# VectorE takes expert 1's branch, the output tiles are cleared by ScalarE and GpSimd in parts, and one written order runs to the end

## The chip, the cores and the metric

One Trainium2 chip, one of its cores. The number that counts is device time in microseconds (us) of one execution; it is given as the median of repeated runs. The core has five engines with instruction queues of their own: TensorE (PE; its weight loads are shown as PEld), VectorE (DVE), ScalarE (ACT), GpSimd (POOL) and SyncE (SP, which here only issues DMAs). Each engine works through its own queue in order, and engines wait for each other with semaphores. In the views of the profile a "q" behind an engine's name (ACTq) marks its sequencer: waits, register loads and branches, in which the engine computes nothing.

## What is computed

A retention layer (a recurrent linear attention with one decay per head) is followed by a mixture of eight experts, of which each token takes one. Cut to what matters:

```python
# attention: q, k, v are (4, 8, 768, 64); gamma = 1 - 2^(-5-h), scale = 1/8
for t in range(S):
    state = gamma * state + outer(k[t], v[t])
    y[t] = scale * q[t] @ state
x = y.transpose(0, 2, 1, 3).reshape(3072, 512)
# experts: w_gate (512, 8), w1 (8, 512, 1024), w2 (8, 1024, 512)
logits = x @ w_gate
expert = argmax(logits, axis=1)
gate_w = softmax(logits)[expert]
out[token] = gate_w[token] * (relu(x[token] @ w1[expert]) @ w2[expert])
```

Which tokens go to which expert is known only on the chip, at run time. All arithmetic that matters for time is float32.

## The kernel before, in words

**Attention and routing.** The first 434 to 735 lines work through 24 steps of 128 tokens. Each step writes its rows of `x` to a scratch array in DRAM (`x_d`), and the routing is worked out beside it: for each expert `e` a list of the rows it must fetch (`src`), of the rows of the output that it must write (`dst`), the gate factors, and the number of its tokens (`ne`). From `ne` comes `arm` (line 421): for each expert, a number that says how many blocks of 8 tokens above 256 it has.

**The early part of expert 0** (lines 737 to 788). The first 256 rows of expert 0 are gathered into `xs2[0]` and computed ahead of the general loop: layer 1 with 256 columns, then `pair` (line 341), which is layer 2 of two token tiles in seven instead of eight products. The result lies in `oa`, the first half of `xs2[0]` itself. Then come, on VectorE, the targets of these rows (`targets(*early, "_e")`, which ends in `dst_e`), the sixteen block transposes that turn the rows of expert 1 into columns (`turn(xs2[1], xT1, ...)`, line 209), and the targets of all rows (`dst`). GpSimd writes the early rows out (`scatter`, line 390).

**Memory that is handed on.** The pools `att` and `keep` of the attention end at line 789. The pools `mp` and `keep2`, which hold `hT`, the output tiles `o2[0]` and `o2[1]`, the second set of weights and the work tiles, take over their memory. So the first user of a new tile on each engine waits until the last user of the old pools is done; that is VectorE's last part of the early `pair` (line 355).

**The loop over the experts** (line 899). Expert `e` has its tokens in four tiles of 128. Three engines may take a branch for it (`tc.Switch`, line 929): there are 33 versions ("arms") of the code, one for each possible number of columns `n`, and a register with `arm[e]` picks one. `regs(e)` (line 406) loads the register; `fetch_ahead` (line 410) gives PE and ACT a hint of the coming arm. Before the change PE and ACT branch for every expert, and DVE from expert 2 on. In an arm lie layer 1 and the part of layer 2 that belongs to tiles 2 and 3 (`layer2`, line 227; for expert 0 the tiles 0 and 1 that the early part left over). After the arms comes `pair` for tiles 0 and 1, whose shape is always the same.

Layer 1 is `layer1` for experts 0 and 1 (line 220): for each of eight blocks `f`, PE makes a product in one of four PSUM buffers (`acc8[2 + f % 4]`), and ACT takes it through Relu into `hT`. So the product of block 4 can't start before ACT has emptied block 0. From expert 2 on it is `quarters1` (line 291), seven products for eight, with sums on DVE and the turns of the next expert spread between them (`spare`).

Beside each expert run: on DVE the sixteen turns of the next expert's rows (`turn`), the four sums of `h` that `pair` needs (`halves_of_h`, line 248, lines 253 to 256 in the profile), and the four sums of `x` for the next layer 1 (`halves_of_x`, line 289); on POOL the gathers of the rows of the expert after next, the scatters of finished rows, and the sums of the weights (`halves_of_w`, line 265; `halves_of_w1`, line 275); on SP the loads of the weights, 2 MB each (lines 150 and 155), into two homes in turn, each as soon as its old content has been used.

**The output tiles** are scattered whole, with rows beyond the expert's tokens sent nowhere. These rows must hold something defined, so both tiles are cleared once by POOL (lines 886 and 887) ahead of the loop.

**What sets the order.** Inside `tc.manual_schedule` the instructions of the named engines stay in the order in which the program writes them. Before the change there are two such stretches, one from line 700 to the end of the attention block, and one from line 885 on. At the seam a scheduler has mixed some instructions of both: ACT's and DVE's register loads stand early, the first clearing stands ahead of the early scatter on POOL, and six instructions of `dst` stand between the first turns of expert 2 on DVE.

Of the kernel before, what the change touches and what calls it, by code (L numbers as in the profile page):

```python
# [17 lines left out]
AF = mybir.ActivationFunctionType  # L18
# [3 lines left out]
P = 128  # L22
# [24 lines left out]
def middle(ap, n):  # L47

    dims = [list(d) for d in ap.ap]
    return bass.AP(tensor=ap.tensor, offset=ap.offset, ap=[dims[0], [0, n]] + dims[1:])  # L50
# [3 lines left out]
def kernel(  # L54
# [11 lines left out]
    nc = tc.nc  # L66
    B, H, S, D = q.shape
    N, DM = out.shape
# [7 lines left out]
    TC = W // P  # L76
# [10 lines left out]
    def ps(tag, bufs, name):  # L87
        return psum.tile([P, 512], F32, tag=tag, name=name, bufs=bufs)

    L = 32  # L90
    Q = P // L
# [6 lines left out]
    ident = const.tile([P, P], F32, tag="ident", name="ident")  # L98
# [54 lines left out]
    def weights2(pool, e):  # L153
        w2t = pool.tile([P, 1, FT, DM], F32, tag="w2t", name="w2t")
        nc.sync.dma_start(w2t, w2v[:, ds(e, 1), :, :])
        return w2t
# [7 lines left out]
    def gather(xs, idx, tiles, rows=N):  # L164
        for t in tiles:
            nc.gpsimd.indirect_dma_start(  # L166
                out=xs[:, t, :], out_offset=None, in_=x_d[0:rows, :],
                in_offset=bass.IndirectOffsetOnAxis(ap=idx[:, t : t + 1], axis=0), bounds_check=rows - 1,
                oob_is_err=False)
# [34 lines left out]
    def turns(xs, xT, tiles, which=range(Q * Q)):  # L204

        n = len(tiles)
        for i in which:
            r, g = divmod(i, Q)
            nc.vector.transpose(  # L209
                xT[ts(g, L), :, 0 : n * P].rearrange("p a (t r i) -> p r t a i", r=Q, i=L)[:, r, :, :, :],  # L210
                xs[ts(r, L), tiles[0] : tiles[0] + n, ts(g, P)].rearrange("p t (a i) -> p t a i", i=L))
            yield

    def turn(xs, xT, tiles, which=range(Q * Q)):
        for _ in turns(xs, xT, tiles, which):
            pass
# [3 lines left out]
    def layer1(n, xT, w1t, hT, f, tags=None):  # L220
        hp = (ps(*tags[f % len(tags)], "hp") if tags else acc8[2 + f % 4])[:, 0:n]
        for dt in range(DT):
            nc.tensor.matmul(hp, lhsT=w1t[:, 0, dt, ts(f, P)], rhs=xT[:, dt, 0:n], start=(dt == 0),  # L223
                             stop=(dt == DT - 1))
        nc.scalar.activation(out=hT[:, f, 0:n], in_=hp, func=AF.Relu)  # L225
# [22 lines left out]
    def halves_of_h(hT, hs, others=nc.vector):  # L248


        hs = [h.rearrange("p (f t) -> p f t", f=FH) for h in hs]
        a11, a12, a21, a22 = (hT[:, ts(j, FH), ts(i, P)] for i in range(2) for j in range(2))
        nc.vector.tensor_tensor(out=hs[0], in0=a21, in1=a22, op=ALU.add)
        nc.vector.tensor_tensor(out=hs[1], in0=hs[0], in1=a11, op=ALU.subtract)  # L254
        others.tensor_tensor(out=hs[3], in0=a12, in1=hs[1], op=ALU.subtract)
        others.tensor_tensor(out=hs[2], in0=a11, in1=a21, op=ALU.subtract)
        return hs
# [141 lines left out]
    PE, ACT, POOL, DVE, SP = (getattr(mybir.EngineType, nm) for nm in ("PE", "Activation", "Pool", "DVE", "SP"))  # L399
# [3 lines left out]
    HALF = EARLY // P  # L403
    ARMS = MOST - LEAST + 1

    def regs(e):
        return {g: nc.engines[g].value_load(arm[0:1, e : e + 1], min_val=0, max_val=ARMS - 1)
                for g in ((PE, ACT) if e < 2 else (PE, ACT, DVE))}

    def fetch_ahead(which, e):  # L410
        tc.switch_hint({g: which[g] for g in (PE, ACT)}, ARMS, label=f"job{e}")
# [22 lines left out]
    with ExitStack() as actx:  # L434
# [262 lines left out]
        LATE = len(steps) - 3  # L697
        for n in range(AHEAD):
            load(n)
        actx.enter_context(tc.manual_schedule(engines={PE, ACT, POOL, DVE, SP}))  # L700
        scale_v = scale(0)
        transpose(0)
        scale_v()
# [89 lines left out]
    o2 = [keep2.tile([P, TC, DM], F32, tag=f"o{i}", name=f"o{i}") for i in range(2)]  # L793
# [88 lines left out]
                layer2(W, hT, w2t, o2[E % 2], t, ogates[:, ts(j, TC)], iter(acc8[6 + t % 2 : 7 + t % 2]))  # L882
            scatter(o2[E % 2], odst[:, ts(j, TC)], range(TC))

    with tc.manual_schedule(engines={PE, ACT, POOL, DVE, SP}):
        for t in o2:
            nc.gpsimd.memset(t, 0.0)
        acc8.extend(ps(tag, n, f"p{i}") for i, (tag, n) in enumerate((("sc", 2), ("sc", 2), ("lg", 1)) + (("tr", 3),) * 3 + (("y", 2),) * 2))
        xT, xTn, rest = xTa, xT1, None
        s3 = [keep2.tile([P, 2, F // 2], F32, tag=f"s{i}", name=f"s{i}", bufs=1) for i in range(3)]  # L890
        T = [keep2.tile([P, 2, W // 2], F32, tag=f"t{i}", name=f"t{i}", bufs=1) for i in range(4)]
        hs = [keep2.tile([P, FH * P], F32, tag=f"hs{i}", name=f"hs{i}", bufs=1) for i in range(4)]
        ws = [keep2.tile([P, FH * DH], F32, tag=f"ws{i}", name=f"ws{i}", bufs=1) for i in range(4)]
        temps = [[keep2.tile([P, W // 2], F32, tag=f"q{k}{i}", name=f"q{k}{i}", bufs=1) for i in range(2)] for k in range(3)]
        turn_of = keep2.tile([P, 1], F32, tag="turn_of", name="turn_of", bufs=1)
        of_pair = dict(m10=temps[0][0], m11=temps[0][1], u20=temps[1][0], u21=temps[1][1], u3=temps[2][0])
        PLACES = (1, 1, 1, 2) * 2

        for e in range(E):
            last = e + 1 == E  # L900
            nxt = None if last else regs(e + 1)

            def hint():
                fetch_ahead(nxt, e + 1)

            hT = mp.tile([P, FT, W], F32, tag="hT", name="hT")
            if e and not last:
                xTn = xT1 if e % 2 == 0 else mp.tile([P, DT, W], F32, tag="xTs", name="xTs", bufs=1)
            xsn = xs2[(e + 1) % 2]

            def layer_one(n):
                if e < 2:
                    for f in range(FT):
                        layer1(n, xT, w1s[e], hT, f)
                    return
                todo, counts = iter(range(Q * Q)), iter(PLACES)

                def spare():
                    k = next(counts)
                    if not last:  # L920
                        turn(xsn, xTn, range(TC), [i for _, i in zip(range(k), todo)])

                rest()
                quarters1(n, xT, w1s[e], S, T, hT, temps, spare)
                halves_of_h(hT, hs)

            if e and e + 2 < E:
                gather(xs2[e % 2], cols[e + 2][0], range(TC))
            for a in tc.Switch(which, ARMS, hint=f"job{e}"):
                n = max(STEP * (LEAST + a) - (0 if e else EARLY), STEP)  # L930
                job(n, xT, w1s[e], w2s[e], hT, o2[e % 2], cols[e][2], HALF if e else 0, lambda: None if e else hint(), layer_one)
            if e > 1:
                scatter(o2[(e - 1) % 2], cols[e - 1][1], [1, 0])
            if e == 0:
                gather(xs2[0], cols[2][0], range(TC))
                scatter(o2[0], cols[0][1], range(HALF))
                w2s.append(weights2(homes[0], 2))
                w1s.append(weights1(homes[0], 2))
                xT, which = xTn, nxt
                continue  # L940
            halves_of_w(w2s[e], ws, by=nc.gpsimd)
            if not last:
                turn(xsn, xTn, range(TC), range(sum(PLACES) if e > 1 else 0, Q * Q))
            if e == 1:
                halves_of_h(hT, hs)
            if not last:
                halves_of_x(xTn, T)
                nc.gpsimd.tensor_copy(turn_of, T[3][:, 0, 0:1])  # L948
                S = halves_of_w1(w1s[e + 1], s3)
                xT, which = xTn, nxt  # L950
            if e + 2 < E:
                w1s.append(weights1(homes[e % 2], e + 2))
            if last:
                more = nc.values_load(over[0:1, 0:1], min_val=0, max_val=1)
            scatter(o2[e % 2], cols[e][1], range(HALF, TC))
            rest = pair(hT, w2s[e], *([x.rearrange("p (f t) -> p f t", f=FH) for x in xs_] for xs_ in (hs, ws)), o2[e % 2], cols[e][2], lambda: None if last else hint(), of_pair.get,
                        late=not last)
            if last:
                with tc.If(more > 0, preferred_fallthrough_block=False):
                    further_jobs()  # L960
                scatter(o2[e % 2], cols[e][1], [1, 0])
            if e + 2 < E:
                w2s.append(weights2(homes[e % 2], e + 2))
# [25 lines left out]
```

## Time and profile before

| | us |
|---|---|
| median of 3 runs | 470.79 (470.25 to 471.63) |
| the execution that was profiled, its time | 474.16 |
| span of that execution, first to last instruction | 472.4 |
| PE busy (matmuls) | 447.4 (95%) |
| DVE busy | 301.1 (64%) |
| POOL busy | 245.8 (52%) |
| ACT busy | 130.5 (28%) |
| attention and routing with the first layer 1 of expert 0, about | 0 to 151 |
| early `pair` of expert 0 | 151.8 to 165.4 |
| arm of expert 0 | 165.3 to 179.5 |
| arm and `pair` of expert 1 | 180.5 to 223.6 |
| experts 2 to 7 | 223.6 to 464 |

A line of the timeline reads: start, duration, engine, line of the kernel, operation, output<-inputs with their shapes, count, and in brackets how long the engine had been idle and who ended that. Matmuls overlap, so a group of them takes a little less than the sum. In this execution expert 0's arm has 104 columns and expert 1's arm 392.

### The profile page before, as it was taken

What the parts mean: (1) busy time and instruction counts of PE and PEld (TensorE: products, weight loads), DVE (VectorE), ACT (ScalarE), POOL (GpSimd) and SP (SyncE); (2) the same over time, 40 slices, a digit from 0 to 9 for tenths busy, and PEclk for the clock granted to TensorE, in tenths of its full rate; (3) what the DMA queues carried; (4) which work ended last, traced back from release to release, by engine and by line L of the source; (5) the groups of instructions that cost most, each with busy time, mean ns of one, the idle gap of its engine ahead of it and who ended that gap; (6) DMA issues with size and microseconds to landing.
All of it is one profiled execution on the core that took longest, in us unless ns stands there. A gap on an engine that the chain in (4) does not pass through costs nothing.

```text
span 472.4 us, 9372 instructions
## 1 busy us (share of the span) xinstructions
PE 447.4 (95%) x3550; PEld 356.0 (75%) x3550; DVE 301.1 (64%) x674; ACT 130.5 (28%) x313; POOL 245.8 (52%) x192
## 2 busy tenths in 40 slices
PE   8998999999799999999999999999999999999992
PEld 4876787777568774558967995897798589689772
DVE  4468697888677792915677557458765748753410
ACT  2553444444321110221231132114222212212310
POOL 2753643450304253486881983787289289169311
PEclk9998999999989999999999999999999999999998
DMA  9998998998941089614714541380563415001001
GB/s 203 222 226 213 209 226 213 213 227 274 276 102 41 4 279 367 239 42 179 262 47 182 156 164 51 137 291 25 182 219 94 176 44 218 5 6 62 3 30 49
DMA packets 93541, 72.74 MB, mean 154 GB/s; under 512 B 53482, under 2 KB 78058, under 8 KB 93424
## 3 DMA queue, kind: packets, MB, share of 16 engines
q1 hardware_dynamic: 88160, 58.74, 44.5%
q0 software_dynamic: 5120, 12.60, 7.7%
q8 instruction: 48, 0.79, 0.7%
q14 instruction: 69, 0.57, 0.4%
q10 hardware_dynamic: 144, 0.05, 0.0%
HBM read 60.88 MB, written 14.68 MB: 160 GB/s over the span
## 4 chain that ended last, share of the span: by engine, by line
PE 77%; DVE 15%; issue 2%; ACT 1%; SPq 1%; DMA 1%; POOL 1%; POOLq 0%; another core or an unknown queue 0%; DVEq 0%; ACTq 0%
PE p L303 21%; PE p L349 17%; PE p L236 12%; PE p L223 5%; PE y L558 4%; PE sc L526 4%; DVE xT L209 4%; PE hp L223 3%; PE tr L473 3%; PE new L537 2%; PE y L554 2%; PE parts L589 2%; DVE am L528 1%; DMA q<-in_q_dram 1%; DVE xTa L209 1%
## 5 line engine op out<-in xcount | busy, mean ns | idle before, releaser
L236 PE MATMUL p<-w2t,hT 128*8 128x128 f32 (+6 forms) x496 | 67.9, 362 | 0.3
L236 PEld LDWEIGHTS p<-w2t,hT 128*8 128x8 f32 (+6 forms) x496 | 31.7, 122 | 32.1 <-issue 27.2
L392 POOL DMA_INDIRECT out_dram<-o,dst x30 | 29.9, 996 | 39.0 <-ACT o L244 12.0
L209 DVE STREAM_TRANSPOSE xT<-xs 32x512 f32<-32x512 f32 x64 | 44.9, 702 | 6.1 <-issue 5.0
L166 POOL DMA_INDIRECT xs<-x_d,src x28 | 29.3, 1047 | 30.8 <-DVE gate_e L201 18.2
L209 DVE STREAM_TRANSPOSE xTs<-xs 32x512 f32<-32x512 f32 x48 | 33.7, 702 | 12.9 <-ACT hT L225 8.9
L528 DVE TENSOR_TENSOR am<-sc,causal 128x512 f32<-128x512 f32 x48 | 30.7, 682 | 17.3 <-PE sc L526 13.7
L485 POOL TENSOR_TENSOR qs<-q,dec 128x512 f32<-128x512 f32 x22 | 22.5, 1045 | 32.7 <-DMA q<-in_q_dram 31.6
L349 PE MATMUL p<-ws,hs 128*128 128x256 f32 x168 | 37.5, 379 | 0.6 <-DVE hs L254 0.6
L490 POOL TENSOR_TENSOR vs<-v,dec 128x512 f32<-128x512 f32 x23 | 23.9, 1044 | 25.7 <-PE y L558 12.2
L303 PE MATMUL p<-t,w1t 128*128 128x196 f32 (+5 forms) x192 | 36.1, 331 | 1.2 <-DVE q L307 1.1
L303 PE MATMUL p<-t,s 128*128 128x196 f32 (+5 forms) x192 | 35.9, 330 | 0.7 <-DVE hT L307 0.7
L349 PEld LDWEIGHTS p<-ws,hs 128*128 128x128 f32 x168 | 31.8, 190 | 5.3 <-issue 1.0
L948 POOL COPY turn_of<-t 128x1 f32<-128x1 f32 x6 | 1.1, 183 | 64.2 <-DVE t L289 64.2
L307 DVE TENSOR_TENSOR hT<-p,q 128x196 f32<-128x196 f32 (+5 forms) x72 | 23.9, 359 | 16.6 <-PE p L303 13.5
L303 PEld LDWEIGHTS p<-t,w1t 128*128 128x128 f32 x192 | 32.3, 190 | 2.1 <-DVE q L307 2.1
L265 POOL TENSOR_TENSOR ws<-w2t,ws 128x1024 f32<-128x1024 f32 x14 | 33.0, 2358 | 0.6
L265 POOL TENSOR_TENSOR ws<-w2t 128x1024 f32<-128x1024 f32 x14 | 33.1, 2364 | 0.1
L303 PEld LDWEIGHTS p<-t,s 128*128 128x128 f32 x192 | 32.4, 190 | 0.9 <-DVE hT L307 0.9
L558 PE MATMUL y<-am,vs 128*64 128x128 f32 x384 | 30.3, 287 | 2.4 <-DVE am L528 2.2
L307 DVE TENSOR_TENSOR q<-p,q 128x196 f32<-128x196 f32 (+5 forms) x48 | 16.2, 360 | 24.3 <-PE p L303 12.9
L355 DVE SCALAR_TENSOR_TENSOR o<-p,gate,q 128x256 f32<-128x256 f32 x21 | 10.0, 483 | 30.6 <-PE p L349 30.2
(204 smaller groups left out, 868.8 us busy)
## 6 DMA issues: line engine op xcount, KB each, us to landing
w1t<-in_moe_w_dram SPq DMA_DIRECT2D x8, 2048.0 KB, 8.3
w2t<-in_moe_w_dram SPq DMA_DIRECT2D x8, 2048.0 KB, 11.1
k<-in_k_dram SPq DMA_DIRECT2D x24, 256.0 KB, 5.1
v<-in_v_dram SPq DMA_DIRECT2D x24, 256.0 KB, 5.7
x_d<-xg SPq DMA_DIRECT2D x24, 256.0 KB, 4.6
q<-in_q_dram SPq DMA_DIRECT2D x11, 512.0 KB, 6.4
q<-in_q_dram SPq DMA_DIRECT2D x2, 256.0 KB, 3.2
out_dram<-o,dst POOLq DMA_INDIRECT x30, 2.8
```

The source lines that it names most:

```text
L166: nc.gpsimd.indirect_dma_start(out=xs[:, t, :], out_offset=None, in_=x_d[0:rows, :], in_offset=bass.IndirectOffsetOnAxis(ap=idx[:, t : t + ...
L209: nc.vector.transpose(xT[ts(g, L), :, 0 : n * P].rearrange("p a (t r i) -> p r t a i", r=Q, i=L)[:, r, :, :, :], xs[ts(r, L), tiles[0] : t ...
L223: nc.tensor.matmul(hp, lhsT=w1t[:, 0, dt, ts(f, P)], rhs=xT[:, dt, 0:n], start=(dt == 0), stop=(dt == DT - 1))
L236: nc.tensor.matmul(y[j * z : j * z + m, 0:c], lhsT=hT[:, f, t * P + r0 : t * P + r0 + m], rhs=w2t[:, 0, f, ts(j, c)], start=(i == 0), stop ...
L265: by.tensor_tensor(out=ws[i], in0=sums[i][0], in1=sums[i][1], op=ALU.subtract)
L303: nc.tensor.matmul(rows(y), lhsT=a(d, f), rhs=b(d), start=start and d == 0, stop=d == 1, skip_group_check=True)
L307: nc.vector.tensor_tensor(out=to, in0=rows(y), in1=rows(plus), op=ALU.add)
L349: nc.tensor.matmul(y, lhsT=a[:, f, :], rhs=b[:, f, :], start=start and f == 0, stop=f == FH - 1, skip_group_check=True)
L392: done = nc.gpsimd.indirect_dma_start(out=out[:, :], out_offset=bass.IndirectOffsetOnAxis(ap=idx[:, t : t + 1], axis=0), in_=o[:, t, :], i ...
L490: mul.tensor_tensor(out=vs, in0=got["v"], in1=inner(dec[:, ts(NC + c, H)], D), op=ALU.mult)
L528: nc.vector.tensor_tensor(out=am[j], in0=sc[j], in1=middle(causal[:, :], HP), op=ALU.mult)
L558: nc.tensor.matmul(place_of(a, j), lhsT=vs[:, 2 * a + j, :], rhs=am[j][:, a, :], start=(c == 0), stop=True, skip_group_check=True)
```

## The change

Four edits, all between the end of the early part and the `pair` of expert 1:

1. VectorE gets a register for expert 1 too, and so a branch there. In each arm of expert 1 it does the sixteen turns of expert 2's rows and the four sums of `h`. Before, both stood behind the arms, in code that is the same for all.
2. The output tiles are cleared in parts. Tiles 0 and 1 of `o2[0]` are set to zero by two ScalarE instructions (a copy of `ident`, spread over the tile, times 0.0); tiles 2 and 3 of both `o2[0]` and `o2[1]` by two GpSimd memsets of half the old size, which now stand behind the arms of expert 0. Tiles 0 and 1 of `o2[1]` are no longer cleared.
3. The hand-written order, which ended with the attention block, now runs to the end of the program.
4. The range of the turns behind the arms is empty for expert 1.

```diff
     def regs(e):
         return {g: nc.engines[g].value_load(arm[0:1, e : e + 1], min_val=0, max_val=ARMS - 1)
-                for g in ((PE, ACT) if e < 2 else (PE, ACT, DVE))}
+                for g in ((PE, ACT) if e < 1 else (PE, ACT, DVE))}
...
-        actx.enter_context(tc.manual_schedule(engines={PE, ACT, POOL, DVE, SP}))
+        ctx.enter_context(tc.manual_schedule(engines={PE, ACT, POOL, DVE, SP}))
...
-    with tc.manual_schedule(engines={PE, ACT, POOL, DVE, SP}):
-        for t in o2:
-            nc.gpsimd.memset(t, 0.0)
+    if True:
+        for h in range(HALF):
+            nc.scalar.activation(out=o2[0][:, h, :].rearrange("p (a b) -> p a b", b=P), in_=middle(ident[:, :], DM // P),
+                                 func=AF.Copy, scale=0.0)
...
                 if e < 2:
                     for f in range(FT):
                         layer1(n, xT, w1s[e], hT, f)
+                    if e:
+                        turn(xsn, xTn, range(TC))
+                        halves_of_h(hT, hs)
                     return
...
             if e == 0:
+                for t in o2:
+                    nc.gpsimd.memset(t[:, HALF:TC, :], 0.0)
                 gather(xs2[0], cols[2][0], range(TC))
...
             if not last:
-                turn(xsn, xTn, range(TC), range(sum(PLACES) if e > 1 else 0, Q * Q))
-            if e == 1:
-                halves_of_h(hT, hs)
+                turn(xsn, xTn, range(TC), range(sum(PLACES) if e > 1 else Q * Q, Q * Q))
             if not last:
                 halves_of_x(xTn, T)
```

In the built program the order on the engines around this place becomes:

- ACT: last part of the early `pair` (line 376), the two clearings, the register load for expert 1 (`regs(1)`), then the branch into expert 0's arm and its eight Relu. Before, that register was loaded earlier, in the midst of the early layer 1, and the branch into expert 0's arm followed line 376 directly.
- DVE: the sixteen turns of expert 1, all eight instructions of `dst`, the register loads, the branch, the sixteen turns of expert 2 and the four sums of `h` in the arm, then `halves_of_x`.
- POOL: the two early scatters, two half clearings, the gathers for expert 2, the scatters of expert 0's rest, and so on as before. Before, a whole clearing stood ahead of the early scatters and another behind them.
- PE and SP: as before, instruction by instruction.

## The prediction

> **What bounds the kernel now.** I read the page first. TensorE is busy 95% of the span, and the chain that ended last is PE for 77%; a change beside PE counts only where PE stands still. So I next read who PE waited for behind the early part (165 us on). There is little to win: five waits, 4.1 us in all.
>
> ```profile
> engine line waited for: us in total, times, longest us
> PE p L303 <- DVE q L307: 1.1, 2, 0.7
> PE p L223 <- DVE at L188: 1.0, 1, 1.0
> PE p L303 <- issue: 0.7, 1, 0.7
> PE p L303 <- DVE hT L307: 0.7, 1, 0.7
> PE p L349 <- DVE hs L254: 0.6, 1, 0.6
> ```
>
> The second and the last lie where the change works: PE's first matmul for expert 1 (it starts at 180.45) and its first product with sums of h (213.14). The other three lie in layer 1 of later experts, which the change doesn't edit.
>
> The timeline of ACT shows where a loss can arise:
>
> ```profile
> 161.99 0.47 ACT L376 ACTIVATE xs<-yp,gate_e 128x256 f32<-128x256 f32 x1 [7.40 <-PE yp L349]
> 166.59 0.26 ACT L225 ACTIVATE hT<-p 128x104 f32<-128x104 f32 x1 [4.12 <-PE p L223]
> ...
> 169.06 0.26 ACT L225 ACTIVATE hT<-p 128x104 f32<-128x104 f32 x1 [0.64 <-PE p L223]
> 169.96 0.26 ACT L225 ACTIVATE hT<-p 128x104 f32<-128x104 f32 x1 [0.64 <-PE p L223]
> ...
> 179.56 0.69 ACT L244 ACTIVATE o<-p,gate 104x512 f32<-104x512 f32 x1 [6.66 <-PE p L236]
> 188.68 1.28 ACT L225 ACTIVATE hT<-p 128x392 f32<-128x392 f32 x3 [8.43 <-PE p L223]
> ```
>
> ACT has 4.1 us between line 376 and the first Relu of expert 0's arm; the two clearings are put there. The views of lines 985 and 929 (the branch, and the first instruction behind it) show that these 4.1 us aren't empty: the branch starts at 162.2 and the arm's first instruction comes at 164.7.
>
> ```profile
> L985 ACTq COMPARE_BRANCH  x1: 62/62/62, 162.2 to 162.2; - x1
> ...
> L929 ACTq BRANCH_PREFETCH_HINT  x1: 36/36/36, 164.7 to 164.7; - x1
> ...
> L985 ACTq COMPARE_BRANCH  x2: 37/57/77, 179.6 to 183.9; - x2
> ```
>
> So a branch of ACT costs 2.5 us here before any work. The same two views put expert 1's branch at 183.9 and the arm at 188.5 (4.6 us), expert 2's at 221.2 and 224.1 (2.9), and the way out of expert 0's arm took from 179.6 to the next register load at 183.1 (3.5). The windows say what differs: the DMA engines were 2% busy from 160 to 166, and nearly full at the two long ones.
>
> ```profile
> 160.00:166.00 6.00, 6.00 (x33) 5.21 (x32) 5.76 (x15) 0.47 (x1) 0.00 (x0) 1.00 0.02 5
> ...
> 168.00:170.00 2.00, 2.00 (x21) 2.00 (x19) 1.88 (x7) 0.56 (x3) 0.42 (x1) 1.00 0.95 334
> ```
>
> (The last two columns are the DMA share and GB/s.) From 167 on the weights of expert 1 stream in, 4.2 MB, released at 166.1.
>
> **The change part by part.**
>
> *ScalarE's clearings: on the path, +3.2 us.* They write memory of the closed pools, so they wait for VectorE's last part of the early pair, which ends at 165.12 + 0.88 = 166.00; the old memset waited for the same and began at 166.15. In the built program the clearing waits for that same count of VectorE. ACT is a queue: behind the waiting clearing stand the second one, the register load for expert 1, the branch, and eight Relu, for which PE waits.
> - First clearing 166.15. Its size is that of line 244 (0.69). Neighbours overlap by about 0.11 (three of 0.50 take 1.28), so the second starts at 166.73.
> - The register load starts with it (line 376 at 220.38, its load at 220.4), and the branch comes 0.8 later (220.4 to 221.2, and 183.1 to 183.9): 167.5.
> - The arm's code: 2.5 us at least (this arm, idle DMA), 4.6 at most (expert 1's arm, full DMA). At 167.5 the DMA is full, so I take the mean of the two loaded rows, (3.5 + 4.6)/2 = 4.1. First Relu, with 0.15 from the arm's first instruction (188.5 to 188.68): 171.75.
> - PE's eight blocks follow each other at 0.90 (169.06 to 169.96), so block 4 starts at 165.25 + 3.6 = 168.85. It reuses block 0's PSUM buffer, and must now wait for 171.75 + 0.26 + 0.1 of signal = 172.1.
>
> So PE stalls 3.25 us in the middle of expert 0's layer 1; with 2.5 for the code 1.65, with 4.6 3.75. Nothing behind it has slack to take that up: layer 2 follows directly on PE, and the second set of weights for expert 2 (line 155, 179.50) is released by it, late by as much, but isn't used before 243.
>
> [...]
>
> [...] At 166.11 two tiny instructions took 1.86 us, while the memset ran (166.15 to 167.96):
>
> ```profile
> 166.15 1.81 POOL L887 MEMSET o<- 128x2048 f32 x1 [9.69 <-DVE at_e L188]
> ```
> ```profile
> 166.11 1.86 DVE L189 TENSOR_SCALAR two_e<-at_e 128x6 int32<-128x6 int32 x1
> ```
>
> Their kind takes 0.17 elsewhere (lines 191, 192). With the memset gone, the turns of expert 1 start and end 1.7 us earlier: 178.5 instead of 180.2. That looks like the cure for PE's 0.98 at 180.45. It isn't alone: PE's branch started at 174.8 and took 4.93 us, and its first instruction in the arm stands at 179.8, followed by five waits of 0.1 each:
>
> ```profile
> L985 PEldq COMPARE_BRANCH  x2: 761/2844/4926, 173.0 to 174.8; - x2
> ```
>
> PE would have begun near 180.4 anyway. With the stall, PE's branch moves to about 178, when the 4.2 MB are all but in (at the 330 to 410 GB/s of the windows, 11 to 13 us from 167), and the next weights can't start before layer 2 ends. Then it may load faster (most PE branches took 0.3 to 0.4, others 2.7 and 3.5). The gap goes or stays: 0 to -0.98; I take -0.5, the middle, as the traffic is ending but not gone.
>
> *The sums of h in the arm: -0.6.* PE waited 0.60 at 212.54, as the sums started at 211.57, behind ACT's last output of the arms (210.85 + 0.69), though hT was complete at 202.3. In the arm they start then and take 1.4 for the first two, 9 us ahead of need. VectorE must be there in time: dst ends near 180, two register loads and the branch follow (3.6 us on DVE at 220.0), the gather lands by 189.35 as before or earlier, and the sixteen turns (0.72 each) end by 201. Even a pause of 4.1 (the longest on VectorE, line 307 <- issue) is covered by the 3.25 that hT comes later. Way out of the arm: under 3 us; it lies before the parts that VectorE owes PE at 215.
>
> *Moved on GpSimd: 0.* Two half clearings (0.9 each) stand where one whole stood, behind the scatters and ahead of the four gathers; these wait for the scatters' landing anyway (176.85). The scatters go 2 us earlier, expert 0's rest some 10 us earlier (dst is no longer between turns; the POOL wait was 10.8), and so the sums of w2 end about 201 instead of 211, those of w1 for expert 2 before 226, where PE first needs one at 224.9 + 2. The memsets run beside turns, which kept 0.70 under the old second memset. Register loads moved off the early layer 1: PE had no wait there.
>
> *Sum:* +3.25 - 0.5 - 0.6 = +2.15. The profiled execution (474.16, span 472.4) would become 476.3; it lies 3.4 above the median of 470.79, so on that scale 472.9.
>
> **The rivals.**
>
> *A, faster: the arm's code is there when ACT branches.* ACT got a hint of the arm at 154.2 and waits from 162.5 to 166; if that time serves the load, the Relu comes before 168.5 and PE doesn't wait. Then -0.6 to -0.6 - 0.98: 470.2 to 469.2, say 469.4. Against it: the hint stood 8 us ahead in the old kernel too, and the branch still cost 2.5.
>
> *B, no change: the load is as quick as before.* 2.5 us, a stall of 1.65, PE's gap gone, sums gained: +0.07, 470.9. For it: most of ACT's branches took 2.5 to 2.9. Against it: the DMA share of 0.95.
>
> *C, slower still: VectorE's new branch comes late.* No hint is given for it, and it falls into the same traffic. If it and a pause in the arm cost more than the 9 us of slack, PE waits in pair of expert 1; it decides from there. At two pauses of 4 us on top of a late gather 2 us would show: 475. For it: line 307's pauses. Against it: the slack.
>
> **How the numbers follow.** Forecast (ACT's late arm) 0.56, A 0.16, B 0.21, C 0.07. The forecast's own range is 470.9 (1.65, gap and sums won) to 474.0 (3.75, gap stays), and PE's four other short stops after 235 (0.4 to 0.75 each) can come or go with shifted code and traffic, about 0.7 either way. Predicted 472.9; with B in and A and C mostly out, 470.3 to 474.7. A measurement of this kernel can tell about 0.3% (1.4 us) from no change. Faster by more: A's better half and a trace of B, 0.12. Within: half of A's rest, most of B and the low end of the forecast, 0.31. Slower: 0.57.
>
> **What would show it.** Right: in expert 0's arm the first Relu comes at 171 to 172.5, PE has a stop of 2 to 4 us between blocks 3 and 4 with ACT as its releaser, and expert 1's first matmul is later than 181.5; the 0.6 at the sums of h is gone; two_e takes 0.2. Wrong: the Relu comes before 168.5, or PE's stop is under 1 us; a wait of PE on hs or on the turns in expert 1 would speak for C. The forecast falls if the code loads while ACT waits.

## The result, and the profile after

The changed kernel is a little faster: 468.68 us in the median of 7 runs (467.12 to 470.77), beside 470.9 us for the kernel before (7 runs, 470.0 to 472.37). The ratio is 0.9945, with a 95% interval of 0.9921 to 0.997. A second, later comparison gave 0.9942 (0.9915 to 0.9969). I had forecast 472.9, so the sign was wrong.

The profiled execution took 470.77 us (span 469.1); it is the slowest of the seven. TensorE's stages, from the starts of its groups in the timelines:

| stage (us) | before | after | difference |
|---|---|---|---|
| start of the span to expert 0's arm | 165.25 | 161.13 | -4.12 |
| layer 1 in expert 0's arm | 7.19 | 13.67 | +6.48 |
| from there to expert 1's first matmul | 8.01 | 6.87 | -1.14 |
| expert 1, arm and `pair` | 43.12 | 42.08 | -1.04 |
| experts 2 to 7, to the end | 248.78 | 245.31 | -3.47 |

The first row can't be credited to the change. In the first profile of the kernel before, VectorE stopped for 3.56 us at 125.6 and TensorE's clock was halved (0.51) from 130.3 to 133.7; over all profiles of this study the arm starts anywhere from 158.4 to 165.3, and one and the same kernel (`e5_h_out` and `r_h_out` below, on two chips) had it at 165.1 and at 160.5. The other rows are the matter of this chapter. The second and third of them start, in the kernel before, at these groups:

```profile
165.25 7.35 PE L223 MATMUL p<-xTa,w1t 128*128 128x104 f32 x64
172.44 7.03 PE L236 MATMUL p<-w2t,hT 128*104 128x512 f32 x16
```

Who TensorE waited for, from 120 to 470 us (engine, line, releaser: total, times, longest), after:

```profile
engine line waited for: us in total, times, longest us
PE p L223 <- ACT hT L225: 3.5, 1, 3.5
PE p L303 <- issue: 1.6, 1, 1.6
```

The first line is the stop that the prediction described. It is now the largest; the waits at expert 1's start and at the sums of `h` are gone from this list. The timeline of the changed kernel shows the stop being made:

```profile
162.04 1.15 ACT L887 ACTIVATE o<-ident 128x512 f32<-128x512 f32 x2 [3.69 <-DVE at_e L188]
...
168.09 0.71 ACT L225 ACTIVATE hT<-p 128x104 f32<-128x104 f32 x4 [4.90 <-issue]
168.40 6.57 PE L223 MATMUL p<-xTa,w1t 128*128 128x104 f32 x32 [3.49 <-ACT hT L225]
```

ScalarE clears, branches at 163.2, and stands idle for 4.90 us until its first Relu; TensorE, which had filled its four PSUM buffers, stops for 3.49. But its next four blocks take 6.57 us, where the old kernel's took 3.6. The windows over this stretch tell why (the number behind the busy times of the five engines is the granted TensorE clock, then DMA share and GB/s):

```profile
161.13:167.37 6.24, 3.78 (x33) 3.61 (x32) 5.99 (x17) 1.15 (x2) 3.23 (x4) 1.00 0.65 221
167.37:174.20 6.83, 5.80 (x27) 5.80 (x28) 6.71 (x10) 1.48 (x7) 2.70 (x3) 0.50 0.99 376
174.20:181.67 7.47, 7.47 (x23) 3.35 (x23) 2.41 (x11) 0.26 (x1) 2.00 (x2) 1.00 0.60 220
```

The clock is 0.50 for 6.83 us, beginning within the stop. So ScalarE's clearings cost this profile 6.5 us in that stage, twice what I had summed, and still the kernel got faster. (In `r_after` and `e3_clear` below the clock is at half for 3.41 us only, and the stage costs 5.3 and 5.4.) Something else pays for it.

### The profile page after: what moved, and what is told of

Read it like the earlier page. It is cut to its first block, busy times and chain, and to the rows that moved or that the text cites. A ratio compares the mean times of both kernels' runs of the same rounds, so it can differ in the third digit from the quotient of the medians.

```text
span 469.1 us, 9377 instructions
## 1 busy us (share of the span) xinstructions
PE 445.9 (95%) x3550; PEld 358.8 (76%) x3550; DVE 301.7 (64%) x674; ACT 132.2 (28%) x315; POOL 244.7 (52%) x192
## 3 DMA queue, kind: packets, MB, share of 16 engines
q0 software_dynamic: 5120, 12.60, 7.6%
## 4 chain that ended last, share of the span: by engine, by line
PE 62%; issue 2%; DVE 2%; ACT 1%; POOLq 0%; ACTq 0%
PE p L303 24%; PE p L349 18%; PE p L236 14%; PE p L223 6%; DVE xTa L209 1%; DVE xs L355 0%; PE yp L349 0%; POOLq L989 0%; ACT o L241 0%; ACT o L242 0%; ACT o L887 0%; DVE u L355 0%; ACT hT L225 0%; ACTq L989 0%; ACTq L887 0%
## 5 line engine op out<-in xcount | busy, mean ns | idle before, releaser
L236 PE MATMUL p<-w2t,hT 128*8 128x128 f32 (+6 forms) x496 | 66.4, 360 | 0.0
L236 PEld LDWEIGHTS p<-w2t,hT 128*8 128x8 f32 (+6 forms) x496 | 32.6, 123 | 29.5 <-issue 26.7
L166 POOL DMA_INDIRECT xs<-x_d,src x28 | 29.3, 1045 | 26.4 <-DVE gate_e L201 14.8
L526 PE MATMUL sc<-qT,kT 64*128 64x128 f32 x384 | 28.8, 291 | 0.7 <-ACT kT L511 0.7
```

Of the source, the lines that this page charges most:

```text
L166: nc.gpsimd.indirect_dma_start(out=xs[:, t, :], out_offset=None, in_=x_d[0:rows, :], in_offset=bass.IndirectOffsetOnAxis(ap=idx[:, t : t + ...
L236: nc.tensor.matmul(y[j * z : j * z + m, 0:c], lhsT=hT[:, f, t * P + r0 : t * P + r0 + m], rhs=w2t[:, 0, f, ts(j, c)], start=(i == 0), stop ...
L526: nc.tensor.matmul(sc[j][:, a, :], lhsT=kT[r, a, :], rhs=qT[r, a, :], start=True, stop=True)
```

## The experiments

Kernels measured together share a chip and the runs of the kernel before; a ratio is always to these.

### The parts of the change, one at a time

`e1_order`, the written order alone:

```diff
-        actx.enter_context(tc.manual_schedule(engines={PE, ACT, POOL, DVE, SP}))
+        ctx.enter_context(tc.manual_schedule(engines={PE, ACT, POOL, DVE, SP}))
...
-    with tc.manual_schedule(engines={PE, ACT, POOL, DVE, SP}):
+    if True:
```

> The kernel before with the one written order alone: expert 1 without VectorE's branch, the output tiles cleared whole by GpSimd as before. Theory 'branch' (the gain comes from VectorE's branch of expert 1 and what it moves in experts 1 to 7): no gain here, ratio to before 0.998 to 1.002, and VectorE's pauses inside the arms of experts 2 to 7 (rows of L307 that wait for issue, 3 to 4 us each) still there. Theory 'order' (the gain comes from the order at the seam, with the register loads off layer 1): ratio 0.985 to 0.992, since here no clearings on ScalarE take any of it back. Theory 'place' (any change of the program's length moves the pauses): the pauses change here too, either way by 1 to 3 us.

`e2_branch`, VectorE's branch alone (edits 1 and 4):

> The kernel before with VectorE's branch of expert 1 alone (its register load, the turns and the sums of h in the arm), the clearings whole on GpSimd and the two written orders as before. Theory 'branch': ratio 0.985 to 0.992 (my two small terms, 1.1 us, and the 3.5 us that the traces show over experts 2 to 7), with no waits of L307 for issue in experts 2 to 7. Theory 'order': ratio 0.997 to 1.000 (1.1 us at most), the pauses still there. Theory 'place': pauses at other places, the ratio between these.

`e3_clear`, the clearings alone (edit 2):

> The kernel before with the clearings alone as in the change (two on ScalarE ahead of expert 0's arm, the halves on GpSimd behind it). All theories: ScalarE enters its arm 4 to 5 us later and TensorE stops for 3 to 3.7 us in layer 1 of expert 0. If that stop alone counts: ratio 1.006 to 1.008. If the clock that falls to half behind it counts too, 3 us more: 1.012 to 1.015. If the ratio is 1.000 +- 0.002, the stop is made good later, and that term of the sum was wrong.

`e4_poolclear`, the changed kernel without ScalarE's clearings:

```diff
-        for h in range(HALF):
-            nc.scalar.activation(out=o2[0][:, h, :].rearrange("p (a b) -> p a b", b=P), in_=middle(ident[:, :], DM // P),
-                                 func=AF.Copy, scale=0.0)
+        nc.gpsimd.memset(o2[0][:, 0:HALF, :], 0.0)
```

> The changed kernel with its two clearings on ScalarE replaced by one memset of the same half tile on GpSimd. If ScalarE's late arm costs what the trace shows (a stop of 3.5 us, and 3.0 us of halved clock behind it): ratio to before 0.980 to 0.988, and neither the stop nor the halved clock at expert 0. If the arm's code comes late whoever clears, or the time is made good later: 0.993 to 0.997, as the changed kernel.

| run | median us | ratio | 95% |
|---|---|---|---|
| e1_order | 469.96 | 0.998 | 0.9959 to 1.0001 |
| e2_branch | 462.79 | 0.9817 | 0.9786 to 0.9849 |
| e3_clear | 475.02 | 1.0084 | 1.0057 to 1.0112 |
| e4_poolclear | 462.22 | 0.9805 | 0.9778 to 0.9832 |

(The kernel before: 470.61.) The branch alone gains 8.6 us here (470.61 x 0.0183), of which my terms had 1.1; it is more than theory "branch" had said (0.985 to 0.992). The clearings alone lose 4.0. By its interval this ratio fits the stop alone (1.006 to 1.008) and not the stop and 3 us more, but the profile shows that the halved clock counts and that part is made good: in e3_clear's profile layer 1 of expert 0's arm takes 12.60 in place of 7.19, and 1.1 of it comes back, as expert 1's first matmul follows after 6.87 in place of 8.01. Without the clearings on ScalarE the changed kernel is as fast as the branch alone: the two intervals overlap, and its median is the lowest here. The order by itself can't be told from nothing. Theory "order" is out. But one thing that "branch" had expected of e1_order did not come: its profile has none of VectorE's stops of some 2 to 4 us inside the arms of experts 2 to 5 (rows of line 307 in the first profile, up to 4.07). It has instead a late way out of expert 4's arm, which is taken up below.

### Which part of the branch

`e5_h_out`: the branch holds the turns only, the sums of `h` go back behind the arms. `e6_h_only`: it holds the sums only, the turns stand ahead of it. `e7_pool_late`: the branch whole, and in expert 2

```diff
+            if e == 2:
+                for _ in range(40):
+                    nc.gpsimd.tensor_copy(turn_of, turn_of)
             halves_of_w(w2s[e], ws, by=nc.gpsimd)
```

> VectorE's branch with the turns in it, the sums of h behind the arm as in the kernel before. Theory 'phase' (the gain comes from the sums of h being done during layer 2 of expert 1, which brings GpSimd's work for expert 2, and with it its whole chain in experts 2 to 7, 8 us forward against TensorE's, so that its sums of w2 no longer run beside VectorE's sums of h): the sums wait for ScalarE's whole arm again, GpSimd's copy into turn_of comes 13 us or more behind layer 2's start in expert 1, ratio to before 0.997 to 1.002. Theory 'place' (VectorE's program is shorter or lies elsewhere once it branches): ratio 0.980 to 0.986 as with the whole branch. Theory 'turns' (the turns in the arm carry it): the same 0.980 to 0.986.

> VectorE's branch with the sums of h alone in it, the turns ahead of the branch. Theory 'phase': ratio 0.980 to 0.986, the whole gain. Theory 'turns': 0.996 to 1.000. Theory 'place': 0.980 to 0.986, too; the run before tells it from 'phase'.

> VectorE's branch whole, and 40 tiny copies on GpSimd once, ahead of its sums of w2 for expert 2: nothing else waits for them there, they only push these sums some 7 us back, beside VectorE's sums of h. Theory 'phase', strong form (a late chain stays late from expert to expert): sums of h of expert 2 and of the experts behind it take 3 to 5 us in place of 2.8, the ratio returns to 0.990 to 1.000. Weak form (only expert 2 pays and GpSimd catches up): 0.982 to 0.988. If GpSimd's time of day does not matter: 0.980 to 0.983, as without the copies.

`before_2` is the kernel before, for a second profile:

> The kernel before, unchanged, for a second profile. If the first profile (474.2 us, 3.3 over the median) held disturbances of its own: VectorE's stop of 3.6 us at the end of the attention and its stops inside the arms (10.3 us on L307) are gone, and in their place the collision of GpSimd's sums of w2 with VectorE's sums of h delays expert 5, as in the two kernels without the branch measured so far. If they belong to the kernel: they recur at the same places.

Measured: before_2 473.0 us (one run); e5_h_out 471.35 us, 1.0013 (0.9985 to 1.0042); e6_h_only 471.06, 1.0009 (0.998 to 1.0039); e7_pool_late 471.27, 1.0009 (0.9971 to 1.0047). None of them has a gain. For e5 and e7 theory "phase" had said so; for e6 it had said the opposite. But this group had run on another chip than e2_branch, and the branch alone was not run there. So by themselves these three can't tell a lost gain from a chip that shows none, and I measured the main ones (not e6) side by side on one chip:

> VectorE's branch alone once more, now beside the kernels it is to be compared with: the runs with the branch whole and the runs with parts of it or with the late GpSimd came from different calls, on different chips. Theory 'phase': 0.979 to 0.985 again, whatever the chip. If the chip made the difference: 0.995 or more here, or the two following at 0.985 or less.

> The branch whole with the 40 tiny copies on GpSimd, again, beside the kernel without them. Theory 'phase', strong form: 0.995 to 1.003, 8 us more than without the copies, which themselves take 7 us of an engine that nobody waits for there. If the chip made the difference: as the kernel without the copies.

> The branch with the turns alone, the sums of h behind the arm, again on the chip of the others. Theory 'phase': 0.997 to 1.003. If the chip made the difference: 0.985 or less.

> The changed kernel again, on the chip of the branch alone. If its clearings cost ScalarE's late arm and the halved clock behind it and nothing else: the branch's ratio plus 0.012 to 0.016, and the time in the stage between layer 1 and layer 2 of expert 0. If the stop alone counts: plus 0.007.

| run (one chip; the kernel before 470.64) | median us | ratio | 95% |
|---|---|---|---|
| r_branch | 464.37 | 0.9869 | 0.983 to 0.9909 |
| r_late | 471.45 | 1.0009 | 0.9979 to 1.0039 |
| r_h_out | 471.1 | 0.9995 | 0.9971 to 1.002 |
| r_after | 468.39 | 0.9942 | 0.9915 to 0.9969 |

The branch gains 6.2 us here, and the changed kernel lies 4.0 above it, by the same account (in its stage 12.51 in place of r_branch's 7.20, then 6.87 in place of 8.40). On this chip, too, the late GpSimd and the sums of `h` behind the arms each take the whole gain away, so for e5 and e7 the chip isn't needed as a cause. r_branch itself came out at 0.9869, beyond the 0.985 that I had set as its limit.

What the gain hangs on can be read at expert 1. The timeline of r_h_out (no gain):

```profile
206.63 0.69 DVE L253 TENSOR_TENSOR hs<-hT 128x512 f32<-128x512 f32 x1 [10.01 <-ACT o L244]
...
211.97 0.18 POOL L950 COPY turn_of<-t 128x1 f32<-128x1 f32 x1 [16.20 <-DVE t L289]
```

and of r_branch (gain):

```profile
196.65 0.69 DVE L253 TENSOR_TENSOR hs<-hT 128x512 f32<-128x512 f32 x1 [0.63 <-ACT hT L225]
...
203.58 0.19 POOL L949 COPY turn_of<-t 128x1 f32<-128x1 f32 x1 [8.10 <-DVE t L289]
```

Behind the arms, VectorE's sums wait for ScalarE's last output of the arm; inside, for the last Relu only. TensorE didn't feel those ten microseconds (its wait was 0.60). GpSimd did: its copy into `turn_of` waits for VectorE's sums of `x` (line 289), which stand behind the sums of `h`, and with it starts GpSimd's chain for the next expert: sums of w1, scatters, gathers, sums of w2 (`ws`), about 29.5 us to their end (203.58 to 233.03 in r_branch). Measured from layer 2's start on TensorE in expert 1 to `turn_of`, all kernels fall into two groups:

| kernels | `turn_of` after layer 2's start | ratio |
|---|---|---|
| before, before_2, e1, e3, e5, r_h_out | 15.1 to 15.3 | 0.998 to 1.001, e3 1.008 (its clearings) |
| e6 | 14.9 | 1.001 |
| e2, r_branch, e4 | 7.6 to 7.8 | 0.980 to 0.987 |
| after, r_after | 7.6, 7.7 | 0.994 (their clearings) |
| e7, r_late | 7.8, 7.6, then pushed in expert 2 | 1.001 |

e6 was not repeated beside r_branch, so its place in this table rests on its profile alone. By that it belongs to the first group, for a reason that I hadn't seen: with the turns ahead of the branch, `dst` is mixed in among them again, GpSimd's scatters and `ws` come late, and `ws` runs beside the sums of `h`. Its timeline:

```profile
199.82 2.37 POOL L265 TENSOR_TENSOR ws<-w2t 128x1024 f32<-128x1024 f32 x1
200.60 2.15 DVE L253 TENSOR_TENSOR hs<-hT 128x512 f32<-128x512 f32 x1 [0.67 <-issue]
...
202.78 2.72 DVE L254 TENSOR_TENSOR hs<-hs,hT 128x512 f32<-128x512 f32 x1
```

A sum that takes 0.69 alone takes 2.1 to 2.8 beside GpSimd's (line 254: 0.69 in r_branch, 2.72 here).

And once late, the chain stays late. In r_late the copies push `ws` of expert 2 beside the sums of `h`:

```profile
236.65 2.15 DVE L253 TENSOR_TENSOR hs<-hT 128x512 f32<-128x512 f32 x1 [0.43 <-ACT hT L339]
...
238.84 2.72 DVE L254 TENSOR_TENSOR hs<-hs,hT 128x512 f32<-128x512 f32 x1
...
241.59 2.72 DVE L255 TENSOR_TENSOR hs<-hT,hs 128x512 f32<-128x512 f32 x1
```

VectorE is late for line 289, `turn_of` comes 17.0 us behind layer 2's start in expert 2 and 15.1 in expert 3 (r_branch: 12.2 and 12.3), and `ws` meets the sums of `h` again in the next expert. From the first of the four sums to the end of the last, in the timelines:

| us | expert 2 | 3 | 4 | 5 |
|---|---|---|---|---|
| r_branch | 2.8 | 2.8 | 3.9 | 6.0 |
| r_h_out | 5.5 | 4.9 | 5.8 | 3.9 |
| r_late | 8.3 | 5.6 | 6.5 | 3.6 |

One push in expert 2 is still there in expert 4, so on this chip the strong form of "phase" holds. In e7, on the other chip, `turn_of` stays late as well (14.8 and 14.9 in experts 3 and 4), but expert 4's sums take 4.0, as in r_branch. In expert 5 r_branch has the longer sums, but its `pair` is only 0.4 longer than r_h_out's (13.07 against 12.69); it is expert 4 that decides.

### Where the late chain costs TensorE its time

Between r_h_out and r_branch the spans differ by 8.60 us, and 7.27 of it lie in one place: from the start of expert 4's `pair` to expert 5's first matmul, 20.23 against 12.96. The timeline of r_h_out there:

```profile
318.69 1.70 DVE L253 TENSOR_TENSOR hs<-hT 128x512 f32<-128x512 f32 x1 [0.42 <-ACT hT L339]
319.80 2.80 POOL L265 TENSOR_TENSOR ws<-w2t,ws 128x1024 f32<-128x1024 f32 x1
320.42 2.73 DVE L254 TENSOR_TENSOR hs<-hs,hT 128x512 f32<-128x512 f32 x1
322.62 0.37 SPq L150 DMA_DIRECT2D w1t<-in_moe_w_dram  x1
...
329.16 4.29 DVE L209 STREAM_TRANSPOSE xT<-xs 32x512 f32<-32x512 f32 x6 [4.68 <-issue]
...
337.70 3.75 PE L349 MATMUL p<-ws,hT 128*128 128x256 f32 x8 [5.11 <-DVE q L355]
```

and of r_branch:

```profile
316.99 1.88 DVE L253 TENSOR_TENSOR hs<-hT 128x512 f32<-128x512 f32 x1 [0.42 <-ACT hT L339]
318.90 0.69 DVE L254 TENSOR_TENSOR hs<-hs,hT 128x512 f32<-128x512 f32 x1
...
320.92 0.37 SPq L150 DMA_DIRECT2D w1t<-in_moe_w_dram  x1
...
322.50 4.30 DVE L209 STREAM_TRANSPOSE xT<-xs 32x512 f32<-32x512 f32 x6 [1.58 <-issue]
...
331.04 1.97 PE L349 MATMUL p<-ws,hT 128*128 128x256 f32 x8
```

In r_branch VectorE is through with the arm (320.92) as the load of expert 6's w1 is issued, and its first instruction behind the arm comes 1.58 later. In r_h_out it ends at 324.48, 1.86 after the issue, and stands for 4.68.

The record of the DMA packets points to what it stands for. Beside the queue of the weights there is one of kind `instruction` (q14). VectorE's jump out of the arm (line 987 in r_h_out, an instruction of its sequencer) is at 323.21, ahead of the end of its last sum, but 0.59 behind the issue of the load. Up to 327.3 only the weights' queue has packets; then come two pieces of 8 KB of the instruction queue, at 327.34 and 327.71, and VectorE goes on at 329.16. The two queues from 323.2 to 328.1 (packets, MB, share of the DMA engines):

```profile
q1 hardware_dynamic: 377, 1.54, 84.9%
q14 instruction: 2, 0.02, 0.8%
```

In r_branch the jump is at 319.64, 1.28 ahead of the issue, the piece comes at 320.66, and VectorE goes on at 322.50. The record doesn't say which engine a piece is for, but at this place all profiles of this study fall into two groups: where the jump is ahead of the load, or there is no load, a piece comes 1.0 to 1.3 us behind the jump and VectorE's stop is 1.5 to 1.8 (thirteen profiles); where the load is ahead, 3.9 to 4.1 and 4.5 to 4.7 (e1_order, e3_clear, r_late, r_h_out).

In r_h_out TensorE then waits 5.11 for VectorE's parts, and a window that begins within this wait has the halved clock (columns as above):

```profile
336.27:339.70 3.43, 2.00 (x5) 1.67 (x6) 1.67 (x4) 0.00 (x0) 3.35 (x3) 0.50 0.01 5
```

That this is a chain of causes, and not three things that happen together, was still only read from their order. Two kernels leave out a link each (and compute something else by it, as their expectations say):

```diff
-            halves_of_w(w2s[e], ws, by=nc.gpsimd)
+            if e != 4:
+                halves_of_w(w2s[e], ws, by=nc.gpsimd)
```

> The kernel before without GpSimd's four sums of w2 for expert 4 (its pair then multiplies expert 3's sums). Theory 'exit' (beside those sums VectorE's sums of h take 6 us in place of 2.8, so VectorE leaves expert 4's arm after the load of expert 6's w1 has been issued, the instructions behind its jump come 4.6 us later in place of 1.5, and TensorE waits 5 us in expert 4's pair, with 3.4 us of halved clock behind it): VectorE out of the arm before the load, its stop there at 1.5 to 1.8 us, ratio to before 0.983 to 0.990. If the chain's late start costs by itself, through what GpSimd does later: 0.997 to 1.002.

```diff
-                w1s.append(weights1(homes[e % 2], e + 2))
+                w1s.append(weights1(homes[e % 2], e + 2) if e != 4 else w1s[4])
```

> The kernel before without the load of expert 6's w1 (its layer 1 then multiplies expert 4's weights). Theory 'exit': the sums of h of expert 4 stay slow, but VectorE's stop behind the arm falls from 4.6 to 1.5 us, TensorE's wait in expert 4's pair from 5 us to 2 or less, ratio 0.986 to 0.993. If the stop has nothing to do with the load: 4.6 us again, and 0.998 to 1.002.

> The changed kernel with the half tile cleared by GpSimd, again on another chip if it comes so: 0.980 to 0.988, as the branch alone or a little better (the one written order gave 0.998 by itself).

| run (one chip; the kernel before 470.43) | median us | ratio | 95% |
|---|---|---|---|
| f_no_ws4 | 464.0 | 0.9837 | 0.9801 to 0.9872 |
| f_no_w6 | 467.01 | 0.9905 | 0.9875 to 0.9936 |
| r_poolclear | 462.43 | 0.9817 | 0.9784 to 0.985 |

f_no_ws4, with expert 1 exactly as in the kernel before and `turn_of` as late as ever (15.1):

```profile
318.97 0.69 DVE L253 TENSOR_TENSOR hs<-hT 128x512 f32<-128x512 f32 x1 [0.42 <-ACT hT L339]
319.70 0.69 DVE L254 TENSOR_TENSOR hs<-hs,hT 128x512 f32<-128x512 f32 x1
...
322.90 0.37 SPq L150 DMA_DIRECT2D w1t<-in_moe_w_dram  x1
323.23 4.30 DVE L209 STREAM_TRANSPOSE xT<-xs 32x512 f32<-32x512 f32 x6 [1.51 <-issue]
```

f_no_w6, with the sums as slow as ever:

```profile
318.85 1.61 DVE L253 TENSOR_TENSOR hs<-hT 128x512 f32<-128x512 f32 x1 [0.42 <-ACT hT L339]
320.49 2.73 DVE L254 TENSOR_TENSOR hs<-hs,hT 128x512 f32<-128x512 f32 x1
...
326.06 4.29 DVE L209 STREAM_TRANSPOSE xT<-xs 32x512 f32<-32x512 f32 x6 [1.51 <-issue]
...
334.60 1.97 PE L349 MATMUL p<-ws,hT 128*128 128x256 f32 x8 [1.84 <-DVE q L355]
```

Both did what theory "exit" said. Without GpSimd's four sums in this one expert VectorE leaves ahead of the load, and 7.7 us are won (470.43 x 0.0163). Without the load the way out takes 1.51 although VectorE comes late (jump at 323.27, the instruction queue's piece at 324.25); TensorE's wait is 1.84 in place of r_h_out's 5.11, no halved clock follows (the eight products behind the wait take 1.97, in r_h_out 3.75), and 4.5 us are won. So one collision on expert 4's sums, and one load that is issued ahead of VectorE's jump, carry nearly all of what the branch gains on the chips whose profiles show the late way out.

The price of the way out is 1.5 to 1.8 us with the weights not in the way and 4.5 to 4.7 behind them. That VectorE stands for the piece of the instruction queue is read from the order of the times alone; that the load makes the difference is shown by f_no_w6 (1.51 in place of 4.68).

## Why the prediction was wrong

- **ScalarE's clearings, +3.25:** the mechanism was right, the size too small. The arm's first instruction came 4.7 us after the branch (4.1 taken), TensorE's stop was 3.49 (forecast 3.25). The first Relu stands at 168.09 only because the whole arm starts 4.1 us earlier in this profile: from the arm's start it is 6.96, where the forecast had 6.5. Left out was the halved clock behind the stop: the stage cost 6.48 (5.3 and 5.4 in r_after and e3_clear). Since the gap at expert 1's start closes in return, the net is 4.0 us (e3_clear alone, and r_after against r_branch), where my terms 3.25 - 0.5 make 2.75. Rivals A (no wait) and B (1.65) are out.
- **PE's gap at expert 1, -0.5 out of 0 to -0.98:** it went whole; the stage is 1.14 shorter. (In its working 4.2 MB at 410 GB/s take 10.2 us, not 11; the middle of 0 and -0.98 doesn't hang on that.) `two_e` took 0.17, as said.
- **The sums of `h`, -0.6:** TensorE's wait of 0.60 is gone, VectorE was there in time, its way out took 1.55 (under 3 forecast). Rival C is out. But the step stopped at TensorE's direct wait. It didn't ask who else stands behind these sums.
- **"Moved on GpSimd: 0": this step failed.** I had worked out that GpSimd's work comes some 10 us forward, and priced it at nothing because TensorE would wait for none of it in expert 1 and 2. What the move is worth is that GpSimd's sums of w2 leave VectorE's sums of `h` alone in the experts behind, so that VectorE jumps out of expert 4's arm ahead of a load and TensorE isn't kept waiting there: with the step above, 6.2 to 8.6 us for the branch in place of 1.1. The "0.7 either way" for the later experts was the same mistake, as it took their stops for chance. The cause is shown where the late way out is seen; for the first pair of profiles it is not (see below).
- **Register loads and order, 0:** 0.998 (0.9959 to 1.0001), no contradiction.

Put together: +4.0 for the clearings, -6.2 to -8.6 for the branch, is -2.2 to -4.6; measured were -2.6 and -2.7 (470.9 x 0.0055, 470.64 x 0.0058).

Was it to be seen beforehand? Not at expert 4. There the profile I read had the kernel before on the good side of the race:

```profile
327.52 0.73 DVE L253 TENSOR_TENSOR hs<-hT 128x512 f32<-128x512 f32 x1 [0.69 <-ACT hT L339]
...
330.81 0.37 SPq L150 DMA_DIRECT2D w1t<-in_moe_w_dram  x1
332.00 4.29 DVE L209 STREAM_TRANSPOSE xT<-xs 32x512 f32<-32x512 f32 x6 [1.69 <-issue]
```

VectorE ended at 330.30, half a microsecond ahead of the load. That execution lost its time elsewhere: layer 1 and 2 of experts 2, 4 and 5 were 4.8 us longer in sum than in r_branch. The changed kernel's profile has none of that, so the -3.47 of the first table comes from there and not from the way out. But a sign of the collision was there to be read: line 253 took 1.89 and 1.67 us in experts 2 and 3, where 0.69 is its time alone.

**Still open.** These longer layers. All four profiles on the chip of e5 to e7 show them as well (3.3 to 4.5 us over experts 2 to 5 in before_2, e5_h_out, e6_h_only and e7_pool_late), and none of these has the late way out; no profile of another chip below has them, and there the kernels with a late chain have the late way out instead (but for f_no_ws4 and f_no_w6, which leave out its links). So how a late chain costs its time on that chip is not shown, and the branch alone wasn't run on it. The kernel before itself was profiled only with the longer layers; that it has the late way out on the other chips is taken from e1_order, which differs from it in the order alone, and from what f_no_ws4 and f_no_w6 won. In the longer layers ScalarE's copies of line 315 and VectorE's sums of line 307 come late (in the first profile the copies at 235.35 and 236.79, 1.44 apart where r_branch has 0.66, and a stop of VectorE of 4.07 up to 238.23), while the rows of TensorE keep their pace there (eight products of 196 columns take 1.49, as in r_branch) and the clock's record says full speed (1.00). Some of VectorE's stops end with the last packets of GpSimd's gathers and scatters (238.23 beside 238.30 in the first profile, 234.98 beside 235.00 in e6), but in r_h_out these packets end as late, 14.7 us behind the start of expert 2's layer 1, without such a stop. I have no cause for it. The expectation for before_2 was wrong twice: the stops inside the arms came again, and the late way out did not come. Nor was the halved clock taken apart from the stop that precedes it.

## What to carry to other kernels

When an engine's work moves, follow it to every engine that waits for it, not to the critical one alone: here a chain that started 8 us earlier kept two engines' sums from running side by side in the experts behind (VectorE's took 0.69 alone, up to 2.8 beside GpSimd's), and a late one held itself late. A stop of the matrix engine can cost more than its length: with the halved clock behind them, stops of 3.4 to 3.5 us made their stage 5.3 to 6.5 longer. And VectorE's first instruction behind expert 4's arm came 4.5 to 4.7 us after its last one in it where a 2 MB load was issued ahead of the jump, 1.5 to 1.8 where it was not, so let the branch go first; clear memory on an engine that nobody waits for (0.9805 and 0.9817, against 0.9945 and 0.9942 with ScalarE doing it, each beside the kernel before).

## What was not expected of the hardware

- In the experts' part, TensorE stops of 3.4 to 5.7 us (after, r_after, e1, e3, r_late, r_h_out) each went with a clock of 0.5, for 3.4 to 6.8 us; stops of 1.6 and 1.84 (after, f_no_w6) did not (1.00 behind the first; behind the second eight products took 1.97, where r_h_out's took 3.75); none lies between.
- The same branch of VectorE out of the same arm took 4.7 us with a 2 MB load issued 0.6 us ahead of its jump, and 1.5 without the load (r_h_out, f_no_w6).
